# Seven products inside one of seven: a second level of the scheme for a12·b21, running sums kept in PSUM, and other steps for the scatters and gathers of the attention stage

## The chip, the cores and the metric

The kernel runs on one core of one Trainium2 chip, as a single program. The metric is the device time of one execution in microseconds (us). Three executions of the kernel before took 925.46, 924.17 and 926.12 us; the median is 925.46 us.

## The reference: what is computed

Two blocks follow each other, both in fp32. First, attention with a threshold, for 8 batches, 8 heads, 576 tokens and 64 features per head; second, a mixture of 8 experts in which a hash of the token's id picks the one expert that handles it.

```python
# attention: q, k, v are (8, 8, 576, 64), tau = 0.02
scores = scale * np.matmul(q, k.transpose(0, 1, 3, 2))
thresh = np.max(scores, axis=-1, keepdims=True) - tau
scores = np.where(scores >= thresh, scores, -1000000000.0)
scores = scores - np.max(scores, axis=-1, keepdims=True)
attn = np.exp(scores)
attn = attn / (np.sum(attn, axis=-1, keepdims=True) + 1e-09)
attn_out = np.matmul(attn, v)
# bridge: x is (4608, 512), a row for each token, the 8 heads side by side
x = attn_out.transpose(0, 2, 1, 3).reshape(B * S, H * D)
# experts: w1 is (8, 512, 1024), w2 is (8, 1024, 512)
expert_idx = token_ids * np.int64(2654435761) % np.int64(E)
for e in range(E):
    xe = x[expert_idx == e]
    out[expert_idx == e] = np.maximum(xe @ w1[e], 0.0) @ w2[e]
```

## The kernel before, in words

**Attention stage.** The work is cut into 32 pairs of heads (4 pairs of heads times 8 batches; index `p`), and each pair into five steps (`NS = 5`, index `s`, running number `n = 5p + s`). Step 0 handles the last 64 queries of both heads together, steps 1 to 4 handle 128 queries of both heads each. For each step TensorE computes scores into PSUM (`score`, L221 to L236), VectorE negates them into SBUF and keeps the row minimum (`negate`, L246), GpSimd adds the threshold to it (`thr`, L253), ScalarE takes the exponential (`expo`, L260), and one step later VectorE zeroes what is below the threshold and sums the rows (`mask`, L271). Two steps later TensorE turns the weights over (`turn_w`, L282), ScalarE copies them out of PSUM (`put_wT`, L298 and L303), and TensorE multiplies them with v (`av_part`, L313). At step 0 the result of the pair before last is turned back (`turn_o`), scaled by VectorE (`put_xm`, L352) and written by SyncE's (SP) queue into a DRAM tensor, `x_scratch` (L358 to L364). The order on every engine is the order of the code in the step loop (L710 to L805): nothing is reordered, so an instruction that waits holds all that is behind it on its engine.

**Routing beside it.** A generator `route` (L366) ranks the tokens in small pieces. When it is far enough (`placed`), `scatters` (L539) starts: 36 indirect DMAs that GpSimd issues, one whenever `next(scatter_pieces)` is called (L800 to L801), which is in steps 0, 2, 3 and 4. Loads of the sorted slots follow. At its end `routed` is set, and `fetch_early` (L677) may gather rows of `x_scratch` for expert 0: 15 indirect DMAs (5 tiles of tokens times the first 3 pairs of heads), one for each call. It is called at the start of step 0 (L713 to L714) and at the end of steps 3 and 4 (L802 to L803), once `n` is above `G0` = 130 (L671). Between the stages TensorE turns the gathered rows over (`early_xT`) and begins expert 0's first layer (`early_h`, `late_h`).

**Expert stage.** Each expert holds up to 600 tokens (544 for expert 0, 576 for experts 1 to 4, 600 for 5 to 7; their halves 272, 288 and 300 are the widths of the matmuls). Both layers are matrix products of 2 by 2 blocks, done with seven block products in place of eight (`seven`, L926): a11·b11, a12·b21, s2·t2, s3·t3, a22·t4, s1·t1 and s4·b22, where s1 to s4 and t1 to t4 are sums of blocks that VectorE makes beforehand (`left`, `right`, L863 to L872). A product is written into a PSUM tile of two banks. Four such tiles go round: two of the pool `ps_sc` and two of `ps_m`, taken in turn by `bank2` (L851). ScalarE copies p1 = a11·b11 to SBUF (L951); VectorE adds the other products to the running sums u2, u3, u4 in SBUF or to the outputs (L861). Layer 1 (L963) is done in two groups of 256 output features, so a12·b21 there is two products of eight matmul instructions each; layer 2 (L972) is one group, and a12·b21 is one product of sixteen instructions. (In the profile an fp32 matmul of the code is two MATMUL instructions, each with its weight load: L941 has four matmuls in a layer-1 product and eight records.) Layer 1 ends with a rectifier on ScalarE (L948).

**What runs beside the products.** `side1` and `side2` (L1093, L1107) hand out the other work after each product: the block sums of the next layer, the 32 by 32 transposes of gathered tokens (`turn_x`, L1060; VectorE then 16 DMAs on SP), the transposes of finished outputs (`put_squares`, L1029; VectorE, then up to ten indirect DMAs on GpSimd, each with a `pause` behind it, L1024: two copies of a small table, L1027, whose result is not read again), the gathers of the expert after next (`fetch`, L1051, with pauses too), and the loads of weights on SP. The weights of layer 2 are dealt (`dealt`, L877): the 128 columns of a weight load lie four elements apart, or two apart for the sums; expert 7's are not. After expert 7's layer 2 come the last 120 tokens (`last_tile`, L983), the last transposes and five indirect DMAs.

The functions that the diff touches and their callers:

## Time and profile before

| What | Value |
|---|---|
| median of three executions | 925.46 us (924.17 to 926.12) |
| the profiled execution, its own time | 926.27 us |
| its span | 924.6 us |
| attention, from the first negation to the end of pair 31's steps | about 7 to 462 us |
| expert 0's first layer, on TensorE | about 464 to 501.8 us |
| products of line L941 | 501.8 to 909.6 us |
| last tile and the last writes | 909.6 to 924.6 us |
| granted TensorE clock, mean | 0.999 |

Busy time is what an engine's instructions cover; the span is from the first instruction to the last. Times of rows in the timeline count from the start of the span. A releaser behind "<-" is what ended an engine's idle time as far as semaphores show it. Two executions of the kernel differ by about 0.1%, and the profiled one lies 0.8 us above the median.

### The profile page before, as it was taken

How to read it: one execution, taken by the hardware profiler on the slowest of the kernel's cores; microseconds unless marked ns; L12 is line 12 of the kernel's file. 1: busy time of each engine (PE TensorE's matmuls, PEld its weight loads, DVE VectorE, ACT ScalarE, POOL GpSimd, SP SyncE). 2: the span in 40 equal slices, each digit the busy share in tenths (PEclk: the TensorE clock that was granted, in tenths of full speed). 3: DMA queues.
4: the chain of work that ended last, by engine and by line, in shares of the span. 5: the costliest groups of instructions: out<-in, count | busy, mean ns of one | idle time of the engine just before them, and what ended most of it. 6: DMA issues, size and time to landing. Idle time of an engine off the chain costs nothing.

```text
span 924.6 us, 21039 instructions
## 1 busy us (share of the span) xinstructions
PE 906.9 (98%) x7495; PEld 661.6 (72%) x7495; DVE 759.9 (82%) x1654; ACT 457.3 (49%) x741; POOL 550.1 (59%) x842
## 2 busy tenths in 40 slices
PE   7999999999999999999999999999999999999997
PEld 4666666656666666565668879788887978879785
DVE  8999999999999999999945696867768685786741
ACT  6888888888888898788922020110202011020210
POOL 4233432456666623446414588787787877878773
PEclk9999999999999999999999999999999999999999
DMA  7454463554545668734011636445252543522001
GB/s 175 95 146 123 107 152 96 134 134 101 124 100 149 167 164 220 209 96 108 16 33 56 195 118 185 136 125 196 63 199 90 170 155 90 218 61 67 28 28 62
DMA packets 114777, 113.13 MB, mean 122 GB/s; under 512 B 32475, under 2 KB 89315, under 8 KB 114672
## 3 DMA queue, kind: packets, MB, share of 16 engines
q1 hardware_dynamic: 105168, 92.64, 37.0%
q0 software_dynamic: 9072, 18.91, 6.6%
q8 instruction: 61, 1.00, 0.4%
q14 instruction: 44, 0.36, 0.1%
q10 hardware_dynamic: 432, 0.21, 0.1%
HBM read 81.99 MB, written 21.44 MB: 112 GB/s over the span
## 4 chain that ended last, share of the span: by engine, by line
PE 83%; POOL 6%; issue 4%; DVE 3%; ACT 2%; DMA 1%; SPq 0%; POOLq 0%; DVEq 0%; ACTq 0%
PE bank L941 18%; PE av L313 18%; PE sc L941 18%; PE sc L235 14%; PE tr L282 11%; POOL out_dram L1042 4%; PE sc L640 3%; POOL stok_odd L1027 2%; PE av L282 1%; DVE ns L246 1%; DVE w L271 1%; ACT w L260 1%; DMA k_sb<-in_k_dram 1%; ACT wT_b L303 1%; PE bank L658 0%
## 5 line engine op out<-in xcount | busy, mean ns | idle before, releaser
L260 ACT ACTIVATE w<-ns,nmx 128x576 f32<-128x576 f32 x288 | 220.4, 776 | 28.6 <-DVE ns L246 27.9
L271 DVE SCALAR_TENSOR_TENSOR w<-ns,thr,w 128x576 f32<-128x576 f32 x288 | 225.7, 816 | 0.0
L253 POOL TENSOR_SCALAR thr<-nmx,drop 128x2 f32<-128x2 f32 (+1 forms) x160 | 104.4, 652 | 188.9 <-DVE ns L246 179.1
L246 DVE TENSOR_SCALAR_CACHE_REDUCE ns<-sc 128x576 f32<-128x576 f32 x288 | 205.7, 746 | 8.5 <-PE sc L235 7.7
L235 PE MATMUL sc<-k_sb,q 64*128 64x288 f32 (+1 forms) x1280 | 178.2, 422 | 1.1 <-DVE ns L246 0.6
L282 PEld LDWEIGHTS tr<-ident,w 64*128 64x128 f32 x2624 | 105.6, 138 | 96.9 <-ACT wT_b L303 35.3
L1042 POOL DMA_INDIRECT out_dram<-o_q,qidx x127 | 139.7, 1100 | 57.8 <-issue 49.2
L282 PE MATMUL tr<-ident,w 64*128 64x64 f32 x2624 | 139.2, 230 | 7.7 <-ACT wT_b L303 4.8
L1027 POOL COPY stok_odd<-stok 128x152 int32<-128x152 int32 x314 | 139.9, 445 | 10.0
L948 ACT ACTIVATE h<-h 128x576 f32<-128x576 f32 (+1 forms) x56 | 38.8, 693 | 142.8 <-DVE h L861 142.0
L235 PEld LDWEIGHTS sc<-k_sb,q 64*128 64x128 f32 (+1 forms) x1280 | 92.2, 177 | 23.5 <-DVE ns L246 9.8
L313 PE MATMUL av<-wT_a,v 128*64 128x320 f32 (+1 forms) x704 | 100.4, 418 | 0.2
L303 ACT COPY wT_a<-tr 128x512 f32<-128x512 f32 (+1 forms) x128 | 81.7, 638 | 20.6 <-PE tr L282 20.1
L303 ACT COPY wT_b<-tr 128x512 f32<-128x512 f32 (+1 forms) x128 | 81.3, 635 | 18.2 <-PE tr L282 10.2
L313 PE MATMUL av<-wT_b,v 128*64 128x256 f32 x640 | 83.2, 389 | 0.0
L313 PEld LDWEIGHTS av<-wT_a,v 128*64 128x64 f32 x704 | 43.7, 136 | 29.0 <-DVE xm L352 0.7
L951 ACT COPY p<-bank 128x576 f32<-128x576 f32 (+2 forms) x11 | 7.0, 634 | 107.5 <-PE bank L941 102.5
L313 PEld LDWEIGHTS av<-wT_b,v 128*64 128x64 f32 x640 | 40.2, 136 | 18.8 <-issue 0.7
L119 POOL DMA_INDIRECT xg<-x_scratch,gidx_x x35 | 41.8, 1193 | 19.2 <-issue 9.3
L542 POOL DMA_INDIRECT slot_scratch<-tok,slot_i x36 | 44.9, 1247 | 9.5 <-issue 7.6
L951 ACT COPY p<-sc 128x576 f32<-128x576 f32 (+2 forms) x11 | 7.0, 637 | 84.7 <-PE sc L941 79.8
L941 PE MATMUL bank<-h,w_sb 128*128 128x288 f32 (+3 forms) x192 | 48.1, 404 | 0.0
(198 smaller groups left out, 1402.4 us busy)
## 6 DMA issues: line engine op xcount, KB each, us to landing
w_sb<-in_moe_w_dram SPq DMA_DIRECT2D x16, 2048.0 KB
q<-in_q_dram SPq DMA_DIRECT2D x62, 288.0 KB
v<-in_v_dram SPq DMA_DIRECT2D x32, 256.0 KB
x_scratch<-xm SPq DMA_DIRECT2D x32, 256.0 KB
xT<-xq SPq DMA_DIRECT2D x84, 80.0 KB
k_sb<-in_k_dram SPq DMA_DIRECT2D x31, 144.0 KB
k_sb<-in_k_dram SPq DMA_DIRECT2D x32, 112.0 KB
x_scratch<-xg SPq DMA_DIRECT2D x9, 256.0 KB
```

Source lines behind the costliest of these rows:

```text
L235: nc.tensor.matmul(sc[out_rows, i, 0:S2], lhsT=q_sb[rows, h, q0:q1], rhs=k_sb[rows, h], start=True, stop=True)
L246: nc.vector.tensor_scalar(out=ns[:].rearrange("p (i s) -> p i s", i=2), in0=sc[:, :, 0:S2], scalar1=-1.0, scalar2=None, op0=ALU.mult, op1= ...
L253: nc.gpsimd.tensor_scalar(out=thr[:, 0:j + 1], in0=stats[n][0][:, 0:j + 1], scalar1=drop[:], scalar2=None, op0=ALU.add)
L260: nc.scalar.activation(w, nss[n, j][:], AF.Exp, bias=stats[n][0][:, j:j + 1], scale=-1.0)
L271: nc.vector.scalar_tensor_tensor(out=w, in0=nss.pop((n, j))[:], scalar=stats[n][1][:, j:j + 1], in1=w, op0=ALU.is_le, op1=ALU.mult, accum_ ...
L282: nc.tensor.transpose(dst[:, r, 64 * c:64 * c + 64], src[rows, c0:c0 + P], ident[rows, rows])
L303: nc.scalar.copy(dst, tr[:, :, 0:64 * n_c].rearrange("p r (c q) -> p r c q", c=n_c))
L313: nc.tensor.matmul(av[64 * j:64 * j + 64, g, c0:c1], lhsT=v_sb[:, c, 64 * j:64 * j + 64], rhs=wT[g][:, i, c0:c1], start=(c == 0), stop=stop)
L542: nc.gpsimd.indirect_dma_start(out=slot_dram[c % 2][:, :], out_offset=bass.IndirectOffsetOnAxis(ap=slot_i[:, c:c + 1], axis=0), in_=tok[:, ...
L941: nc.tensor.matmul(ps[:, i, 0:width], lhsT=lhsT, rhs=y[:, c], start=c == 0, stop=c == n_k - 1)
L1027: nc.gpsimd.tensor_copy(stok_odd[:], stok[:])
L1042: inst = nc.gpsimd.indirect_dma_start(out=rows[:, :], out_offset=bass.IndirectOffsetOnAxis(ap=idx, axis=0), in_=o_sb, in_offset=None, boun ...
```

## The change

Five things change together.

1. `Quarters`: the product a12·b21 of every layer of experts 1 to 7 is itself cut into 2 by 2 blocks and done by seven products of half the width (136 to 150 columns, 120 in expert 7's second layer). Its sums are made by VectorE in `inner_w` (in place and in `wi_s`) and `inner_b` (`bi_s`); for dealt weights ScalarE first copies a12 to a contiguous tile `w2_q` (`copy_quarters`). In layer 1 the two groups' products a12·b21 become one `Quarters` of 28 instructions; expert 0 keeps the plain product.
2. Sums in PSUM: in `Seven` and `Quarters`, u2 = p1 + s2·t2, u3 and c21 are added up by matmuls that go on writing into the tile that holds the earlier sum (`start=False`), after ScalarE or VectorE has copied the intermediate value out of it. c12 goes on in s1·t1's tile in the same way. The tile u4 goes away, and the four PSUM tiles get fixed roles (`banks`).
3. The step lists of `side1` and `side2` are new; `put_squares(e, 0)` moves from step 3 of layer 2 into the middle of its last product, and for expert 0 into expert 1's layer 1.
4. `pause` makes one copy, not two. Outputs of the last tiles use the gather tiles `xg_bufs`, not a pool of their own.
5. In the attention stage, the scatters are issued in steps 0 to 3 (before: 0, 2, 3, 4), and `fetch_early` is called at the end of steps 2 and 3, and of step 4 in pairs 25 and 26 alone. `G0` is 125, so the first gather is at n = 127 (before 133) and the fifteenth at n = 157, step 2 of pair 31 (before 155, step 0 of pair 31).

The core of the diff:

```diff
         LAST = NS * NP
-        G0 = NS * ((HP - 1) * B + 2)
+        G0 = NS * ((HP - 1) * B + 1)
         early = [(kt, hp) for kt in range(KT) for hp in range(HP - 1)]
...
-                if s == 0:
-                    fetch_early(n)
                 if s == 0 and p + 2 < NP:
...
-                if s != 1 and placed:
+                if s < NS - 1 and placed:
                     next(scatter_pieces, None)
-                if s > 2:
+                if s in (2, 3) or s == 4 and n < G0 + 2 * NS:
                     fetch_early(n)
...
-        w2_s = m_s.tile([P, 3, FH, D2], FP32, name="w2_s")
+        w2_s = m_s.tile([P, 2, FH, D2], FP32, name="w2_s")
+        w2_q = m_s.tile([P, 4, 2, P], FP32, name="w2_q")
...
+        banks, turn = [], [2]
...
+        def bank2():
+            turn[0] += 1
+            return banks[(turn[0] - 1) % 4]
...
-            t = triple(w2_s, 0, FH)
-            return t if e == E - 1 else [dealt(x, C2) for x in t]
+            t = [w2_s[:, i] for i in range(2)]
+            if e == E - 1:
+                return [*t, w_tiles["s4"]]
+            return [*(dealt(x, C2) for x in t), w2_blocks(e, w_tiles[e, 2])[1]]
...
-        def seven(a, a_s, b, b_s, m0, outs, relu, after):
...
+        def products(ps, x, y, start, mid=None):
+            for i, lhsTs in enumerate(x):
+                for c, lhsT in enumerate(lhsTs):
+                    nc.tensor.matmul(ps[:, i], lhsT=lhsT, rhs=y[:, c], start=start and c == 0,
+                                     stop=c == len(lhsTs) - 1, skip_group_check=not start)
+                if i == 0 and mid:
+                    mid()
...
+            def first(self):
+                products(self.x, self.a[0], self.b[0], True)
+            def keep_p1(self):
+                nc.scalar.copy(self.p1, self.x)
+            def second(self, y):
+                y = y[:, :, 0:self.x.shape[2]]
+                products(y, self.a[1], self.b[2], True)
+                self.out(self.outs[0], y, self.p1)
+            def u2_sum(self):
+                products(self.x, self.a[4], self.b[4], False)
+                nc.scalar.copy(self.u2, self.x)
+            def s1_t1(self, keep):
+                products(self.z, self.a[2], self.b[1], True)
+                if keep:
+                    nc.scalar.copy(self.mid, self.z)
+            def u3_sum(self, keep):
+                products(self.x, self.a[5], self.b[5], False)
+                if keep:
+                    nc.scalar.copy(self.mid, self.x)
+            def c21(self):
+                products(self.x, self.a[3], self.b[6], False)
+                if self.relu:
+                    nc.scalar.activation(self.outs[2], self.x, AF.Relu)
+                else:
+                    nc.scalar.copy(self.outs[2], self.x)
+            def c12(self, mid=None):
+                products(self.z, self.a[6], self.b[3], False, mid)
+                self.out(self.outs[1], self.z, self.u2)
+            def c22(self, ps):
+                self.out(self.outs[3], ps, self.mid)
+            def c11(self, p1):
+                self.out(self.outs[0], p1, self.outs[0])
...
+            def p1_p2(self):
+                products(self.x, self.a[0], self.b[0], True)
+                nc.scalar.copy(self.p1, self.x)
+                products(self.y, self.a[1], self.b[2], True)
+            def c11(self):
+                add(self.outs[0], self.y, self.p1)()
+            def p5_u2(self):
+                products(self.z, self.a[2], self.b[1], True)
+                nc.scalar.copy(self.p5, self.z)
+                products(self.x, self.a[4], self.b[4], False)
+                nc.scalar.copy(self.u2, self.x)
+            def c12_c22(self):
+                products(self.z, self.a[6], self.b[3], False)
+                add(self.outs[1], self.z, self.u2)()
+                products(self.x, self.a[5], self.b[5], False)
+                add(self.outs[3], self.x, self.p5)()
+            def c21(self):
+                products(self.x, self.a[3], self.b[6], False)
+                nc.scalar.copy(self.outs[2], self.x)
...
+        def copy_quarters(e):
+            w = w2_blocks(e, w_tiles[e, 2])[1]
+            nc.scalar.copy(w2_q[:].rearrange("p (i j) k m -> p i (j k) m", i=2),
+                           w.rearrange("p k m i -> p i k m"))
+        def w2_quarters(e):
+            if e == E - 1:
+                return w_quarters(w2_blocks(e, w_tiles[e, 2])[1])
+            return [w2_q[:, i] for i in range(4)]
...
+        def second_blocks(e, layer):
+            if layer == 1:
+                return w_quarters(w1_blocks(w_tiles[e, 1])[1]), x_blocks(e)[2]
+            return w2_quarters(e), h_blocks(0, FH, half2(e))[2]
+        def quarters_of(e, layer, x, y, z):
+            a_q, b = second_blocks(e, layer)
+            t = b.shape[2] // 2
+            if layer == 1:
+                outs = [h_0[:, 2 * i:2 * i + 2, t * k:t * k + t] for i in range(2) for k in range(2)]
+            else:
+                outs = [oT[:, i:i + 1, t * k:t * k + t] for i in range(2) for k in range(2)]
+            if (e, layer) == (E - 1, 2):
+                a_q[2] = w_tiles["s1_q"]
+            return Quarters(a_q, wi_sums(a_q[0]), b_quarters(b), bi_sums(b), outs,
+                            3 - layer, x, y, z)
...
+            q = quarters_of(e, 1, *banks[1:])
+            g0, g1 = group(0, banks[0], banks[2]), group(1, banks[1], banks[3])
+            w_tiles.pop((e, 1))
+            g0.first()
+            g0.keep_p1()
+            side(0)
+            q.p1_p2()
+            q.c11()
+            g0.u2_sum()
+            side(1)
+            q.p5_u2()
+            g0.s1_t1(True)
+            side(2)
+            q.c12_c22()
+            side(3)
+            g0.u3_sum(False)
+            q.c21()
+            g0.c22(g0.x)
+            side(4)
+            g0.c12()
+            g0.c11(g0.p1)
+            g1.first()
+            g0.relus()
+            side(5)
+            g1.c11(g1.x)
+            g1.relus()
+            g0.c21()
+            side(6)
+            g1.u2_sum()
+            side(7)
+            g1.s1_t1(True)
+            side(8)
+            g1.u3_sum(False)
+            side(9)
+            g1.c22(g1.x)
+            g1.c12()
+            g1.relus()
+            side(10)
+            g1.c21()
...
+            o = Seven(a, w2_sums(e), h_blocks(0, FH, half), triple(h_s, 0, FH, half), 0, outs,
+                      False, *((banks[0], banks[1]) if e else (banks[3], banks[2])))
+            o.first()
+            o.keep_p1()
+            if e == 0:
+                o.second(banks[0])
+                run(w2_first)
+                side(0)
+                o.u2_sum()
+                side(1)
+                o.s1_t1(True)
+                side(2)
+                o.u3_sum(False)
+                o.c22(o.x)
+                side(3)
+                o.c12()
+                side(4)
+                o.c21()
+                return
+            q = quarters_of(e, 2, *(banks[i][:, 0:1] for i in (2, 3, 3)))
+            q.p1_p2()
+            q.c11()
+            run(inner_b(second_blocks(e, 2)[1]), 4)
+            o.u2_sum()
+            q.p5_u2()
+            side(0)
+            o.u3_sum(True)
+            side(1)
+            q.c12_c22()
+            o.s1_t1(False)
+            side(2)
+            q.c21()
+            o.c11(o.p1)
+            o.c22(o.z)
+            o.c21()
+            side(3)
+            o.c12(lambda: side(4))
...
         def pause():
-            for _ in range(2):
-                nc.gpsimd.tensor_copy(stok_odd[:], stok[:])
+            nc.gpsimd.tensor_copy(stok_odd[:], stok[:])
...
-            run(sums_w2(0), 4)
+            w2_first = sums_w2(0)
+            run(w2_first, 3)
...
+            late_h(late_tile)
+            for _ in range(2):
+                banks += [ps_sc.tile([P, 2, 512], FP32, name="sc"),
+                          ps_m.tile([P, 2, 512], FP32, name="bank2")]
...
+                    a, b = second_blocks(e, 2)
...
+                    w2_work += inner_w(a, None if more else w_tiles["s1_q"])
+                    def side1(step):
+                        if step == 0 and e == 1:
+                            put_squares(0, 0)
+                        if step == (0 if e > 1 else 4):
+                            put_squares(e - 1, 1)
+                        if step == 2 and more:
+                            copy_quarters(e)
+                        run(w2_work, ((0, 1, 2, 0, 3, 1, 1, 0, 0, 0, 0) if e > 1 else
+                                      (0, 1, 2, 0, 0, 0, 1, 0, 1, 1, 0))[step])
+                        run(h_work, 2 if step in (8, 9) else 0)
+                        run(turns, ((0, 0, 0, 0, 0, 0, 1, 2, 1, 1, 1) if e > 1 else
+                                    (0, 0, 0, 0, 0, 1, 1, 1, 1, 2, 0))[step])
                     layer1(e, side1)
                     run(sums_h(e, 2, FH), 4)
...
+                    x_work = [sums_w1(e + 1), sums_x(e + 1), inner_w(a), inner_b(b)]
+                    if e == 0:
+                        x_work[1:3] = x_work[2:0:-1]
+                    x_work = sum(x_work, [])
...
-                    else:
-                        run(x_work, 2)
+                    run(x_work, ((1, 2, 3, 10, 0) if e else (2, 2, 0, 4, 8))[step])
                     if step == 2 and e + 2 < E:
                         fetch(e + 2)
                     if step == 4 and e + 2 < E:
                         load_w1(e + 2)
-                    if more and step == 3:
+                    if more and e and step == 4:
                         put_squares(e, 0)
```

Of the parts that are cut: `columns` picks the 128-column weights of a product; `left` and `right` are unchanged; `w_quarters` and `b_quarters` cut a block in four. A layer-1 product of `Seven` is eight instructions, a layer-2 product sixteen, and every product of `Quarters` four.

## The prediction

> **What bounds the kernel now.** I read the page's busy shares first, then busy times by stretch, the chain of work that ended last in order of time, the groups by form, and the timeline of single pairs.
>
> ```profile
> PE 906.9 (98%) x7495; PEld 661.6 (72%) x7495; DVE 759.9 (82%) x1654; ACT 457.3 (49%) x741; POOL 550.1 (59%) x842
> ...
> PEclk9999999999999999999999999999999999999999
> ```
>
> TensorE (PE) covers the span at full clock. The stretches of one expert's two layers show no gap at all:
>
> ```profile
> 602.00:627.00 25.00, 25.00 (x104) 22.00 (x104) 16.24 (x22) 2.69 (x4) 20.21 (x32) 1.00 0.55 160
> 627.00:653.00 26.00, 26.00 (x109) 21.59 (x108) 21.62 (x25) 2.70 (x4) 19.08 (x29) 1.00 0.40 136
> ```
>
> The columns are PE, PEld, DVE, ACT, POOL: PE 100%, DVE 65 to 83%, ACT 10%. In the chain's order of time the products follow each other without a break:
>
> ```profile
> 609.27 3.88 PE sc L941 x16
> 613.15 3.88 PE bank L941 x16
> ...
> 636.43 1.94 PE bank L941 x8
> 638.37 1.94 PE sc L941 x8
> ```
>
> So here an instruction costs its pitch: 3.88/16 = 1.94/8 = 242.5 ns at width 288. The same chain gives 252.5 at 300 (2.02/8), 229.4 at 272 (3.67/16), and the starts of expert 7's layer 2 give 202.5 at 240. All are width/1.2 + 2.5 ns. What is taken from PE in this stage is won, if no wait takes its place.
>
> In the attention stage DVE and PE are both nearly full. A pair takes 13.89 us, from one pair's first L246 row to the next's, in pairs 23 to 26. Pairs 14 to 22, which have scatters, take 14.35 on average (14.19 to 14.65), and pairs 27 to 30, with gathers, 15.96, 14.26, 14.11 and 15.78. Pair 27 in the timeline:
>
> ```profile
> 386.77 1.35 POOL L119 DMA_INDIRECT xg<-x_scratch,gidx  x1 [0.17 <-issue]
> ...
> 388.43 1.02 POOL L119 DMA_INDIRECT xg<-x_scratch,gidx  x1 [0.30 <-issue]
> ...
> 389.49 0.81 POOL L253 TENSOR_SCALAR thr<-nmx,drop 128x1 f32<-128x1 f32 x1
> 389.89 0.58 ACT L303 COPY wT_b<-tr 128x512 f32<-128x512 f32 x1 [1.81 <-PE sc L235]
> ...
> 390.53 0.52 PE L282 MATMUL tr<-ident,w 64*128 64x64 f32 x10 [1.58 <-ACT wT_b L303]
> ...
> 393.81 0.76 DVE L246 TENSOR_SCALAR_CACHE_REDUCE ns<-sc 128x576 f32<-128x576 f32 x1 [1.30 <-PE sc L235]
> ```
>
> The gathers of steps 4 and 0 run back to back over the start of step 0. ACT's wait for a turn that PE finished about 388 ends only at 389.8, then PE is 1.58 us late and DVE 1.30. Pair 30 looks the same. With scatters, the growth sits in step 0 alone: 3.2 us between its negation and the next, against 2.89, and only after a scatter in step 4; scatters in steps 2 and 3 leave their steps at 2.16 and 2.42, as in pair 23.
>
> **What the Trainium skill says.** "TensorE: Matmul & The Clock Gate", LDWEIGHTS (loading the stationary operand): a load takes its 128 columns / 1.2, so 107 ns, whatever the rows, and it overlaps matmuls. The trace agrees: after a break two loads start 108 ns apart (906.23, 906.34), and the last tile's 128-wide matmuls with 120-column weights run at 109 ns. The page has no price for dealt weights; these rows have:
>
> ```profile
> L941 PEld LDWEIGHTS bank<-h,w_sb 128*128 128x128 f32 x192 | 46.7, 300 | 0.5
> ...
> L941 PEld LDWEIGHTS bank<-xT,w_sb 128*128 128x128 f32 x168 | 31.9, 190 | 9.5
> ```
>
> Four elements apart lengthen a load from 190 to about 308 ns, and expert 0's products with such weights have a pitch of 233.75 (3.74/16) where 229.4 is normal: 234 is the load's own pace. "PSUM — Partial Sum Buffer", The four PSUM rules: a synchronised read of a sum in the middle of its group is allowed. No run here shows it yet. "SBUF — State Buffer" has GpSimd and VectorE share a port; the trace can't split that from a wait.
>
> **The change, part by part.** The sum stands against the profiled execution, 926.27 us (span 924.6 plus 1.7 around it), 0.8 above the median.
>
> *Quarters.* Per layer, 16 wide instructions go and 28 narrow ones come. At width 144 I extrapolate 144/1.2 + 2.5 = 122.5 ns (bounds: 121 by proportion; 190, a load's whole record, if loads don't overlap; the 109 ns row excludes the latter). Experts 1 to 4: 16 x 242.5 - 28 x 122.5 = 3.88 - 3.43 = 0.45 us a layer, eight layers, 3.6. Width 150: 4.04 - 28 x 127.5 = 0.47, five layers, 2.35. Expert 7's second: 3.24 - 28 x 109 = 0.19. Sum **-6.1** (bounds -6.7 and -5.5).
>
> *Dealt weights after a narrow product.* In layer 2, s1·t1 and a22·t4 begin behind 122 ns matmuls with a 234 ns load: 2 x 0.11 x 6 experts = **+1.3** (0 to 1.5). The narrow products themselves use contiguous w2_q. That copy, 1024 elements, is about 1.1 us of ACT (row L303: 585 ns for 512, 692 for 640), which is idle there.
>
> *Sums in PSUM.* Now PE waits for a copy before it adds on. Layer 1: after p1, PE has 4 + 4 narrow instructions, 0.98 us. ACT starts 0.24 after PE's last (638.21 to 638.45), copies 0.63 (row p) and PE follows 0.05 later: 0.92. It fits by 0.06 us, but the next weight load can no longer be ahead, so up to 0.11 shows. Layer 2 has this twice (p1, and u2 under p5 and u2 of the quarters). Three places by seven experts by 0.06: **+1.2** (0 to 2.3). The other reads are DVE's. I laid out expert 2 by hand: products at the pitches above, DVE items at 0.75 (adds), 1.22 (w sums), 2.26 (put_squares) and 0.69 (turn_x), the new quarter sums at 0.3 to 0.45 in proportion. Latest are the reads before q.c21 (1.3 us in hand), g1.u2_sum (0.8) and g1.c21 (0.9). None stalls; expert 1, with both put_squares in its layer 1, is about 0.4 late once: **+0.4** (0 to 1.5). Behind such a wait stands all of PE. DVE's load hardly changes: seven adds a group become three, and 16 quarter sums come.
>
> *Start of expert 0's layer 2.* Its first product goes into banks[3], the tile of late_h's last output. DVE reads that at 501.83 for 0.72, while PE is free at 501.80: **+0.85** (0 to 1). The fourth w2 sum moves behind the second product, and no PE work waits for it before c12.
>
> *Pauses, o_sb tiles.* One 445 ns copy less per row: POOL's rows come every 1.6 us, not 2.1. POOL stands in the chain late (839 to 905), but the last output waits for ACT at 918.0, POOL having been free from 917.5: 0. The writes are denser; weights have one expert's time to land. put_squares(e, 0) moves past load_w1 and one product: 2.3 us of DVE ahead of c12's add, 10 indirect DMAs later on POOL, under the next layer's first product; without that cover 2 us each. Expert 0's two blocks go to steps 0 and 4 of expert 1's layer 1, behind which DVE's w2 sums wait; the 0.4 above holds them. turn_x's 16 DMAs leave SP about 23 us into layer 1, 0.6 each, and their first reader comes 15 us into layer 2: 0.
>
> *Expert stage: -6.1 + 1.3 + 1.2 + 0.4 + 0.85 = -2.4.*
>
> *Scatters to step 1.* 36 x 1.25 us of POOL stay. Step 4's growth, 0.33 to 0.46 in each of nine pairs, 4.1 in all, can go. Step 1 on POOL: rec 0.5, scale_k 0.75, thr 0.73, then the scatter, with thr of step 2 queued behind it and DVE's mask behind that, a step later; from pair 26's rows it ends (380.0) before that thr is ready (about 380.6). If it costs what step 4's did, nothing is won. I take **-2** (-4.1 to 0).
>
> *Gathers.* Those of step 0 and three of five in step 4 go to steps 2 and 3, where a DMA of POOL costs nothing in the rows. The excess of pairs 27 to 30 is 2.07 + 0.37 + 0.22 + 1.89 = 4.55; two gathers in step 4 stay (0.35 each); half a us for what is left: **-3.3** (-4.5 to 0). New is that a gather follows the x_scratch writes of step 0 by two steps, not three: in pair 30 SP issues them 4 us into the pair, the gather comes about 8.5 in. The fifteenth, in step 2 of pair 31 (about 455), is needed at 464.8.
>
> Total -2.4 - 2 - 3.3 = **-7.7**: 926.3 - 7.7 = 918.6 profiled, 917.8 as a median; I say **918**.
>
> **The rivals.**
> (A) The sum holds: 918, between 913.5 and 922.5. For it: PE's pitch law and the fitting ledger.
> (B) The attention stalls stay, because SP's loads at step 0, or POOL's work wherever it is put, cause them: 925.5 - 2.4 = 923. For it: the named releaser, PE, had long been done, so the cause isn't seen; pairs 29 and 31 have gathers in step 0 and lose almost nothing.
> (C) Slower: PE is tied to DVE in layer 1. Before, a product had three other tiles' time (over 5.8 us) before its tile was needed; now g1.u2_sum and g1.c21 have 0.8. If DVE's items run 10% longer beside POOL (x_s 0.92 against 0.76 at 629.4 is such a case), the list up to these reads, some 12 us, is 1.2 late: 0.4 at each, and as much at q.c21 and in layer 2, plus the three copies at 0.3: 2.5 us an expert, 17.5 in all, 925.5 - 7.7 + 17.5 = 935. It decides from 1.4 us an expert on (7.7 + 1.9 over seven).
> (D) No change: a gain and stalls of 0.8 to 1.3 us an expert cancel, 925.5.
>
> **How the numbers follow.** Chances: A 0.57, B 0.17, C 0.15, D 0.11. The bounds add up to -6.7 to +0.8 in the expert stage and -8.6 to 0 in attention; all of them at their best would be 910, which I don't expect at once. A, B and half of D fill 912.5 to 925.5, with about 0.8 of the chance; C and the rest are left out. A measurement tells 0.2%, 1.85 us, from no change. Faster by more: A, and B but for 0.03: 0.72. Within: D and that, less a little: 0.12. Slower: C and a little of D: 0.16.
>
> **What would show it.** Right: narrow instructions at 122 to 128 ns; PE without gaps over 0.15 us from 503 on; an expert's two layers (288 wide) in about 53.8 us, before 54.3; a gap of 0.8 at expert 0's first product; pairs 14 to 22 near 13.95, and 27 to 30 near 14. Wrong: PE waiting for DVE's h L861-type adds by over 1 us an expert, narrow instructions above 140 ns, or step 0 still at 3.2 us with scatters in step 1.

## The result, and the profile after

| | before | after |
|---|---|---|
| median, us | 925.06 (9 executions, 923.99 to 926.43) | 919.05 (9 executions, 917.92 to 922.48) |
| ratio, 95% interval | | 0.9945 (0.9931 to 0.9959) |
| profiled execution, us (span) | 926.27 (924.6) | 919.58 (918.0) |
| pairs 14 to 22, over nine times 13.89 | 4.12 | 1.51 |
| pairs 25 to 30, over six times 13.89 | 4.56 | 4.12 |
| from pair 31's start to the end ("the last stage" below) | 477.35 | 473.37 |

The forecast was 918.0, so the total is hit within 1.1 us, and in part by luck: its two halves aren't. The expert stage was to give 2.4 us and gave about 4.0; attention was to give 5.3, and in the profiled executions pair 31 starts 2.7 us earlier (444.6 against 447.3; the pairs of the table won 3.0). The two misses, 1.6 and 2.6 us, have opposite signs. The page of the kernel after, busy times and clock, and the group of the pause (at the right: busy us and mean ns):

```profile
PE 902.9 (98%) x7663; PEld 669.3 (73%) x7663; DVE 758.8 (83%) x1720; ACT 514.0 (56%) x848; POOL 489.8 (53%) x685
...
PEclk9999999999999999999999999999999999999999
...
L1232 POOL COPY stok_odd<-stok 128x152 int32<-128x152 int32 x157 | 71.3, 454 | 0.6
```

PE has 168 instructions more and 4.0 us less to do; ACT has 56.7 us more, most of it copies out of PSUM; POOL lost half its pauses. Busy times by stretch over two experts' 54 us each (columns PE, PEld, DVE, ACT, POOL):

```profile
604.00:658.00 54.00, 54.00 (x251) 47.29 (x250) 40.97 (x59) 15.40 (x26) 37.04 (x45) 1.00 0.45 143
658.00:712.00 54.00, 54.00 (x251) 47.29 (x250) 40.78 (x59) 15.42 (x27) 40.15 (x49) 1.00 0.47 147
```

PE is still without a gap, DVE at 76%, where the kernel before had 74% in the first of these stretches (39.91 us). Layer 2 of expert 2 in the timeline, PE alone (start, duration, instructions):

```profile
609.28 0.65 PE L937 MATMUL sc<-h,w_q 128*128 128x144 f32 x4
609.77 0.65 PE L937 MATMUL bank<-h,w_q 128*128 128x144 f32 x4
610.26 4.07 PE L937 MATMUL sc<-h_s,w_s 128*128 128x288 f32 x16
614.17 0.66 PE L937 MATMUL bank<-h,w_q 128*128 128x144 f32 x4
614.66 0.65 PE L937 MATMUL sc<-bi_s,wi_s 128*128 128x144 f32 x4
615.15 4.12 PE L937 MATMUL sc<-h_s,w_s 128*128 128x288 f32 x16
619.11 0.65 PE L937 MATMUL bank<-h,wi_s 128*128 128x144 f32 x4
619.60 0.65 PE L937 MATMUL sc<-bi_s,wi_s 128*128 128x144 f32 x4
620.09 4.15 PE L937 MATMUL bank<-h,w_sb 128*128 128x288 f32 x16
624.07 0.66 PE L937 MATMUL sc<-bi_s,w_q 128*128 128x144 f32 x4
624.57 4.15 PE L937 MATMUL sc<-h_s,w_sb 128*128 128x288 f32 x16
628.55 0.65 PE L937 MATMUL bank<-h,w_sb 128*128 128x288 f32 x2
```

Read the starts: durations overlap. Four narrow instructions take 0.49 us (609.28 to 609.77), 122.5 ns each. The wide products with dealt `w_sb` behind narrow ones take 3.98 (620.09 to 624.07, 624.57 to 628.55), where 16 x 242.5 ns is 3.88. The two running sums take 3.91 and 3.96.

In attention, the waits of the kernel after in pairs 25 to 27 (us in total, times, longest) show what wasn't there before:

```profile
POOL xg L119 <- DVE ns L246: 15.0, 5, 5.5
...
DVE w L271 <- POOL thr L253: 4.0, 3, 1.8
```

DVE waits for a threshold that POOL computes, and POOL waits up to 5.5 us with a gather. POOL's timeline in pair 25 (which begins at 357.2):

```profile
363.83 0.73 POOL L253 TENSOR_SCALAR thr<-nmx,drop 128x2 f32<-128x2 f32 x1 [1.43 <-DVE ns L246]
369.37 1.13 POOL L119 DMA_INDIRECT xg<-x_scratch,gidx  x1 [4.81 <-DVE ns L246]
370.55 0.31 POOL L253 TENSOR_SCALAR thr<-nmx,drop 128x2 f32<-128x2 f32 x1
371.02 1.65 POOL L119 DMA_INDIRECT xg<-x_scratch,gidx  x1 [0.17 <-issue]
```

The gather of step 2 stands at POOL's head from 364.6 to 369.4, with the threshold of step 3 queued behind it. The releaser named (DVE) had long been done, so another wait was meant. A gather reads `x_scratch` and so waits for the pair's writes to it. SP issued those at 362.0 and they landed about 368.4; SP's own waits from 350 to 403 us say why they were late:

```profile
SPq L358 <- DMA xg<-x_scratch,gidx: 7.8, 2, 4.0
SPq L212 <- DMA w_sb<-in_moe_w_dram: 5.2, 2, 3.1
```

The second row is a load of `v` that, as the profile has it, waits in SP for the weights' DMA, and the writes stand behind it; the first is the writes themselves waiting for the gathers of the pair before, so late gathers in one pair also delay the next pair's writes. The 2 MB load of weights was issued at 352.8, ahead of all of them. From here my theory: these loads cost the gathers their gain. Rivals: two steps are too few for the writes whatever else is in the queue; or the gathers' own work on POOL is the cost.

### The profile page after: what moved, and what is told of

Same layout as the page of the kernel before. It is cut to its first block, busy times and chain, and to the rows that moved or that the text cites. A ratio compares the mean times of both kernels' runs of the same rounds, so it can differ in the third digit from the quotient of the medians.

```text
span 918.0 us, 21463 instructions
## 1 busy us (share of the span) xinstructions
PE 902.9 (98%) x7663; PEld 669.3 (73%) x7663; DVE 758.8 (83%) x1720; ACT 514.0 (56%) x848; POOL 489.8 (53%) x685
## 4 chain that ended last, share of the span: by engine, by line
PE 49%; POOL 27%; issue 15%; DVE 3%; ACT 2%; SPq 1%; DMA 1%; POOLq 1%; DVEq 0%; ACTq 0%
PE av L313 18%; POOL out_dram L1247 16%; PE sc L235 15%; PE tr L282 11%; POOL stok_odd L1232 8%; POOL xg L119 3%; PE sc L640 3%; PE av L282 1%; SPq L1277 1%; ACT w L260 1%; DMA k_sb<-in_k_dram 1%; DVE ns L246 1%; ACT wT_a L303 1%; DVE w L271 1%; POOLq L1247 0%
## 5 line engine op out<-in xcount | busy, mean ns | idle before, releaser
L1247 POOL DMA_INDIRECT out_dram<-o_q,qidx x127 | 147.2, 1159 | 114.4 <-DVE o_q L1238 81.2
L253 POOL TENSOR_SCALAR thr<-nmx,drop 128x2 f32<-128x2 f32 (+1 forms) x160 | 100.2, 626 | 173.9 <-DVE ns L246 162.4
L1232 POOL COPY stok_odd<-stok 128x152 int32<-128x152 int32 x157 | 71.3, 454 | 0.6
L937 PE MATMUL bank<-h,w_sb 128*128 128x288 f32 (+4 forms) x248 | 62.0, 402 | 0.0
L937 PEld LDWEIGHTS bank<-h,w_sb 128*128 128x128 f32 x248 | 58.7, 290 | 0.5
L937 PE MATMUL sc<-h_s,w_s 128*128 128x288 f32 (+2 forms) x224 | 56.6, 406 | 0.0
L961 ACT ACTIVATE h<-h 128x576 f32<-128x576 f32 (+1 forms) x42 | 29.0, 692 | 41.4 <-DVE h L864 36.3
```

The costliest lines, as they stand in the source:

```text
L253: nc.gpsimd.tensor_scalar(out=thr[:, 0:j + 1], in0=stats[n][0][:, 0:j + 1], scalar1=drop[:], scalar2=None, op0=ALU.add)
L937: nc.tensor.matmul(ps[:, i], lhsT=lhsT, rhs=y[:, c], start=start and c == 0, stop=c == len(lhsTs) - 1, skip_group_check=not start)
L1232: nc.gpsimd.tensor_copy(stok_odd[:], stok[:])
L1247: inst = nc.gpsimd.indirect_dma_start(out=rows[:, :], out_offset=bass.IndirectOffsetOnAxis(ap=idx, axis=0), in_=o_sb, in_offset=None, boun ...
```

## The experiments

They ran on three chips, called A, B and C. "Last stage" is from pair 31's start to the end in the profiled execution; it is free of the attention stage. "14-22" and "25-30" are these pairs' time above 13.89 us each, in the same execution. The executions of the section before are called those of the first chip.

| run | chip | median us | ratio to before, same chip (95%) | 14-22 | 25-30 | last stage |
|---|---|---|---|---|---|---|
| before | B | 925.59 | | 3.11 | 4.46 | 477.5 |
| after | B | 918.20 | 0.9914 (0.9894 to 0.9934) | 2.21 | 4.05 | 473.8 |
| after, old scatter steps | B | 920.74 | 0.9941 (0.9923 to 0.9959) | 3.60 | 3.83 | 473.3 |
| after, old gather steps | B | 918.53 | 0.9921 (0.9903 to 0.9938) | 1.22 | 4.19 | 473.6 |
| before | A | 918.21 | | | | |
| after, all old steps | A | 914.54 | 0.9959 (0.9945 to 0.9973) | -0.01 | 0.30 | 473.6 |
| before, new steps only | A | 920.90 | 1.0026 (1.0015 to 1.0037) | -0.01 | 2.18 | 477.6 |
| after, early weights | A | 913.71 | 0.9952 (0.9939 to 0.9966) | 0.00 | 0.16 | 473.3 |
| after, eight products | A | 925.27 | 1.0074 (1.0060 to 1.0088) | -0.01 | 3.16 | 480.0 |
| before | C | 918.14 | | | | |
| after, early weights | C | 913.96 | 0.9956 (0.9942 to 0.9969) | 0.01 | 0.15 | 473.7 |
| after, delay before c11 | C | 935.20 | 1.0189 (1.0174 to 1.0205) | -0.01 | 1.58 | 492.9 |
| after, delay behind c11 | C | 926.58 | 1.0105 (1.0081 to 1.0129) | 0.01 | 0.60 | 484.0 |
| after, two pauses | C | 929.41 | 1.0109 (1.0085 to 1.0132) | 0.01 | 3.75 | 489.2 |

**All steps old, and the steps alone (chip A).**

```diff
-        G0 = NS * ((HP - 1) * B + 1)
+        G0 = NS * ((HP - 1) * B + 2)
...
+                if s == 0:
+                    fetch_early(n)
...
-                if s < NS - 1 and placed:
+                if s != 1 and placed:
...
-                if s in (2, 3) or s == 4 and n < G0 + 2 * NS:
+                if s > 2:
```

> The kernel after with the scatters and gathers put back to their old steps. If the attention stage gave what its pairs show (pairs 14 to 22 won 2.6 us, pairs 25 to 30 won 0.4), this loses 3.0 us: about 922. If the attention stage gave what I had forecast (5.3), 924.3; if the whole gain is the expert stage's, 919. Pairs 25 and 26 should be back at 13.9 us, pair 27 at about 16.

The second kernel is the one before with the same lines the other way round.

> The kernel before with only the new steps of scatters and gathers. Theory (the two stages add up): 925.1 - 3.0 = 922. Rival (the moved transfers help only because expert 0's work then starts in another place, or hurt the expert stage): 925 or 919. Pairs 25 to 27 should show the new stalls in step 4 here too (about 1.3, 0.9 and 1.9 us), since the weights' loads are the same.

Both went against every number that I had given: on this chip the kernel before takes 918.2, the old steps are the faster ones (914.5), and the new steps alone make the kernel before 2.7 us slower. What holds is the sum of parts. The last stage is 473.6 with the new expert stage and 477.6 with the old, as in the first traces (473.4, 477.35), so the expert stage gives 4.0 us on either chip. The new steps' stalls come with the new steps: pair 27 takes 16.05 us in the second kernel, pairs 25 and 26 13.9. The old steps' stalls are missing here: pairs 14 to 22 take 13.89 each, pair 27 takes 14.04 and pair 30 13.89.

What differs can be seen in one place. ACT and POOL near 202.5 us, kernel before, first chip:

```profile
202.44 0.78 ACT L260 ACTIVATE w<-ns,nmx 128x576 f32<-128x576 f32 x1
203.74 0.58 ACT L303 COPY wT_b<-tr 128x512 f32<-128x512 f32 x1 [0.53 <-PE sc L235]
```

```profile
202.14 1.30 POOL L542 DMA_INDIRECT slot_scratch<-tok,slot_i  x1 [0.17 <-issue]
```

The same two engines with all old steps on chip A:

```profile
202.34 0.78 ACT L260 ACTIVATE w<-ns,nmx 128x576 f32<-128x576 f32 x1
203.11 0.59 ACT L303 COPY wT_b<-tr 128x512 f32<-128x512 f32 x1
```

```profile
202.03 1.30 POOL L542 DMA_INDIRECT slot_scratch<-tok,slot_i  x1 [0.17 <-issue]
```

POOL issues the same scatter at the same time, and PE's turn begins its last instruction at 202.88 in the first and 202.79 in the second. ACT's copy of it begins 0.86 us after that in the first and 0.32 in the second. Over pairs 14 to 22, ACT, when it has waited, begins such a copy 0.32 us after the turn's last instruction begins wherever POOL issues no indirect DMA at that moment; where it issues one, the median is 0.65 (at most 1.19) in the kernel before on the first chip, 0.62 on chip B, and 0.32 (at most 0.32) with the same steps on chip A. In the kernel after on the first chip, which still loses 1.5 us in pairs 16 to 21, it is 0.53.

The trace also records when PE's semaphore, its signal to the others, was raised. In the first execution the signals of three PE instructions that ended at 202.86, 203.11 and 203.65 came almost together, at 203.57, 203.66 and 203.72, just after POOL's DMA had ended at 203.44. On chip A they came at 202.78, 203.03 and 203.58, each within 0.03 us of its instruction's end, while POOL's DMA ran until 203.34. So ACT isn't slow: PE's signal itself is late while POOL issues an indirect DMA, on the first chip and on B, and on A and C it isn't. Why is open. Each of A, B and C was used in one set of runs only, so the chip can't be told from anything else that differed between the sets.

**Weights early (chips A and C).**

```diff
-                if s == 2 and p in (20, 24):
-                    load_w1(p // 4 - 5)
-                if s == 2 and p in (22, 26):
-                    load_w2((p - 22) // 4)
+                if s == 2 and p in (16, 20):
+                    load_w1(p // 4 - 4)
+                if s == 2 and p in (18, 22):
+                    load_w2((p - 18) // 4)
```

> The kernel after with the four 2 MB weight loads of experts 0 and 1 four pairs earlier (pairs 16, 18, 20, 22 for 20, 22, 24, 26), so that none shares the DMA queue with gathers. Theory (the x_scratch writes that the gathers of pairs 25 to 27 wait for stand behind a 2 MB load in the queue): writes land within about 5 us of the pair's start, pairs 25 to 27 go back to 13.9 us, 4.1 us are won, 915. Rival 1 (a gather two steps after the writes is too early whatever the queue carries, since SP issues the writes behind the pair's own loads): unchanged, 919. Rival 2 (the loads only move their stalls to the pairs with scatters): pairs 16 to 22 lose what pairs 25 to 27 win, 918 to 919.

Pairs 25 to 27 took 13.89, 13.89 and 14.05 us, pairs 16 to 22 stayed at 13.89: 913.71, and the five executions lie between 913.61 and 914.25. POOL in pair 25 of this kernel:

```profile
361.88 0.73 POOL L253 TENSOR_SCALAR thr<-nmx,drop 128x2 f32<-128x2 f32 x1 [1.43 <-DVE ns L246]
363.97 1.13 POOL L119 DMA_INDIRECT xg<-x_scratch,gidx  x1 [1.36 <-issue]
365.15 0.94 POOL L253 TENSOR_SCALAR thr<-nmx,drop 128x2 f32<-128x2 f32 x1
366.25 1.09 POOL L119 DMA_INDIRECT xg<-x_scratch,gidx  x1 [0.16 <-issue]
367.83 0.71 POOL L253 TENSOR_SCALAR thr<-nmx,drop 128x2 f32<-128x2 f32 x1 [0.50 <-DVE ns L246]
```

The same gather in the same step now begins 2.1 us after the threshold's start, not 5.5, and in SP's own waits the row `SPq L212 <- DMA w_sb` is gone. SP issues pair 25's writes 2.9 us into the pair, not 4.9, and they have landed 7.7 us into it, not 11.2. The theory's 915 had assumed a chip where after takes 919; what shows it right is pairs 25 to 30, with 0.16 us of stalls against 2.18 and 3.16 in the two runs on this chip that have the new gather steps and late weights. Both rivals fall: two steps are enough when the queue is free, and pairs 16 to 22 lose nothing. POOL's own work for the gathers costs at most 0.16 us here; where PE's signals are late this wasn't tried. Over all runs with new gather steps and late weights the stalls range from 0.60 to 4.12 us, presumably with when the 2 MB land against a pair; that would fit the spread of after, 917.92 to 922.48.

> The kernel after with the four early weight loads four pairs earlier, once more, for the chip of this call. Where before takes 918: 913.7, as measured. Where before takes 925: pairs 25 to 27 lose their stalls (4 us in after), the scatters' rest in pairs 16 to 21 stays (1.5 to 2 us): about 914.5 to 915, a ratio to before of 0.989.

The repeat came to chip C, where before takes 918.14: 913.96. On a chip where before takes 925 this version wasn't tried. The gain over all old steps is small where the signals are in time: 913.71 against 914.54 on chip A.

**Eight products in the quarters' block (chip A).** The edit, for layer 1 and layer 2 alike; `inner_w` and `inner_b` write their sums to tiles that nothing reads, ACT's copies of intermediate values go, and DVE copies results where it added (not shown):

```diff
-                products(self.x, self.a[0], self.b[0], True)
-                nc.scalar.copy(self.p1, self.x)
-                products(self.y, self.a[1], self.b[2], True)
+                products(self.y, self.a[0], self.b[0], True)
+                products(self.y, self.a[1], self.b[2], False)
...
+                products(self.z, self.a[0], self.b[1], True)
+                products(self.z, self.a[1], self.b[3], False)
...
+                products(self.x, self.a[2], self.b[1], True)
+                products(self.x, self.a[3], self.b[3], False)
...
+                products(self.x, self.a[2], self.b[0], True)
+                products(self.x, self.a[3], self.b[2], False)
```

> The kernel after with the quarters' block made of eight narrow products, two added up in each PSUM tile, in place of seven with inner sums; DVE's inner sums stay as work whose results nothing uses. PE gets 4 more instructions in each of 13 layers: 8 x 4 x 122.5 + 4 x 4 x 127.5 + 109 x 4 and so on, about 6.4 us, less 0.5 for the copies that nothing waits for now. Theory (expert stage bound by PE's pitch): 919.05 + 5.9 = 925. Rival (DVE bounds the layer since the change): 919 to 921.

The last stage went from 473.4 to 480.0, +6.6. I had counted 13 layers, there are 14: 56 narrow instructions more, eight layers at 122.5 ns, five at 127.5 and one at 109, are 6.9 us, from which go the waits that the copies may have caused. So in this stage added PE instructions cost nearly all of their time, and the rival, DVE, doesn't set the pace. The total, 925.27, looks like the forecast, but by chance: it assumed 919 for after, which on this chip would be about 917 (an estimate, see below).

**After, before, and one half of the steps each (chip B).**

> The kernel after, unchanged, next to the kernel before on the chip of this call. In the last call the kernel before took 918.2, not 925.1, and its old steps stalled nowhere (pairs 14 to 22 at 13.89, pair 27 at 14.04, pair 30 at 13.89), while the new steps kept their stalls in pairs 25 to 27. Theory 1 (the old steps' stalls belong to the chip, the new steps' to the kernel): where before takes about 918, after takes 918.2 - 3.7 (the expert stage) + 2.7 (new stalls) = 917.2, a ratio of 0.999; where before takes 925, 919. Theory 2 (after gains 0.55% wherever it runs): 913 where before takes 918.

> The kernel before, unchanged, for its profile on the chip of this call. If it takes about 918, Theory 1 expects pairs 14 to 22 at 13.89 us and pairs 27 to 30 near 13.9, and ACT's copy of a turned w beginning 0.1 to 0.2 us after PE's turn; if it takes 925, the stalls shown before (14.35 on average, 15.96 and 15.78) and that copy beginning only when PE's four score products have ended.

Chip B is of the kind where before takes 925, so theory 1's 919 applies: 918.20, a ratio of 0.9914. The six executions lie between 915.74 and 920.80, and theory 2's 0.55% would give 920.5 here, so this run doesn't decide between the two; chip A's runs speak for theory 1. The trace of before has the old stalls again (pair 27 15.97 us, pair 30 15.71).

```diff
-                if s < NS - 1 and placed:
+                if s != 1 and placed:
```

> The kernel after with the scatters alone back in their old steps (0, 2, 3, 4). On a chip where before takes 925: 2.6 us slower than after, in pairs 14 to 22. Where it takes 918: no difference from after (below 0.3 us), since the old steps stalled nothing there.

920.74 against 918.20: 2.5 us slower, near the 2.6 expected. But the executions overlap (919.43 to 922.14 against 915.74 to 920.80), so the size is uncertain. In pairs 14 to 22 the profiled executions with old scatter steps lose 3.11 and 3.60 us, those with new ones 2.21 and 1.22: the new steps win something there, 0.9 to 2.4 us.

```diff
-        G0 = NS * ((HP - 1) * B + 1)
+        G0 = NS * ((HP - 1) * B + 2)
...
+                if s == 0:
+                    fetch_early(n)
...
-                if s in (2, 3) or s == 4 and n < G0 + 2 * NS:
+                if s > 2:
```

> The kernel after with the gathers alone back in their old steps (3, 4 and 0, from one pair later on). Where before takes 918: 2.7 to 3.5 us faster than after, pairs 25 to 27 at 13.9 to 14.05, about 914.5. Where it takes 925: 0.4 us slower than after, the stalls in pairs 25 to 27 gone and those in 27 and 30 back.

918.53 against 918.20: no difference that these executions can show (expected 0.4). Pairs 25 and 26 are back at 13.89, pairs 28 and 30 at 15.41 and 15.78 (expected 27 and 30). On such a chip the gathers' new steps exchange one stall for another.

**How much PE has in hand at a DVE result (chip C).**

```diff
+            def extra():
+                w = min(half2(e - 1), half2(e))
+                for _ in range(2):
+                    add(h_s[:, 2, :, 0:w], h_s[:, 0, :, 0:w], h_s[:, 1, :, 0:w])()
...
+            extra()
             g1.c11(g1.x)
```

> The kernel after with two more DVE additions (0.75 us each, from parts of h_s into another part of it that nothing reads before it is written again) in each expert's layer 1, right before g1.c11, the addition that PE's g1.u2_sum waits for. In the trace of after DVE ends g1.c11 0.75 us before PE begins that product (expert 3: 648.71 and 649.46). Theory (in layer 1 PE has that much in hand at this read and no more): 1.5 - 0.75 = 0.75 us an expert, seven experts, +5.3 us in the stage from pair 31 to the end (473.4 in after), about 478.7. Rival (DVE's spare time, over 15% of the stage, takes it up as it did with the old order): 473.4.

935.20, far over the forecast. DVE and PE at that place:

```profile
649.98 2.85 DVE L864 TENSOR_TENSOR h_s<-h_s 128x1152 f32<-128x1152 f32 x2
652.75 0.75 DVE L864 TENSOR_TENSOR h<-bank,h 128x576 f32<-128x576 f32 x1
```

```profile
649.57 2.10 PE L937 MATMUL sc<-x_s,w_sb 128*128 128x288 f32 x8
653.56 0.76 PE L937 MATMUL bank<-x_s,w_s 128*128 128x288 f32 x2 [1.89 <-DVE h L864]
```

My edit was twice as large as I wrote: each addition had 1152 elements and 1.4 us, 2.85 together. Less the 0.75 in hand that is 2.1, and PE's eight instructions, due to last 1.94 us, are followed after 3.99: 2.05 late. The seven experts give 1.99, 2.06, 2.05, 2.09, 1.77, 1.88 and 1.38. The theory holds, at the right size. The stage lost more than these 13.2 us, 19.5, and most of the rest goes to the clock. Busy times by stretch around the stalls of experts 1, 2 and 6 (columns as above, PE's first; the third number from the end is the granted clock):

```profile
538.11:541.53 3.42, 1.91 (x8) 1.54 (x9) 3.42 (x5) 1.23 (x2) 3.25 (x3) 1.00 0.06 19
592.73:596.14 3.41, 1.52 (x7) 0.90 (x6) 3.38 (x4) 0.21 (x2) 3.17 (x3) 1.00 0.12 38
596.14:599.55 3.41, 3.41 (x8) 2.42 (x9) 3.31 (x7) 1.02 (x2) 3.07 (x5) 0.50 0.12 38
599.55:602.97 3.42, 3.42 (x15) 2.68 (x15) 2.63 (x4) 1.28 (x2) 3.13 (x4) 1.00 0.06 19
824.84:828.25 3.41, 1.70 (x8) 0.97 (x7) 3.38 (x6) 1.19 (x2) 3.07 (x4) 1.00 0.06 19
828.25:831.66 3.41, 3.41 (x15) 2.60 (x14) 3.31 (x6) 0.97 (x3) 3.07 (x5) 1.00 0.12 38
```

In the second row PE idles 1.89 us (0.16 less than it is late, since records of neighbouring instructions overlap by that). For the next 3.41 us it runs at half its pace, some 480 ns an instruction, which costs another 1.7 to 1.9 us. The same follows the stalls of experts 3 and 4. In expert 6 PE idles 1.71 us, and the clock stays. Expert 1's stall is longer, 1.83 us of idle, but it falls on two such stretches, 1.51 in the one shown, and the clock stays too; the last section has more on this.

> The same two additions one place later, right behind g1.c11. The next DVE result that PE waits for is c22's addition, read before g1.c21: DVE is busy from 648.97 to 655.10 without a pause, idles 0.45, and ends that addition 0.91 us before PE needs it. Theory: 1.5 - 0.45 - 0.91 = 0.14 us an expert at most, with the signal's time 0.2, so 1.0 to 1.4 us in all, stage 474.4 to 474.8. If the place doesn't matter, the same as the run before (478.7); if neither has a cost, 473.4.

The same call one line later cost 10.6 us in the last stage, against 19.5; the 474.8 at most that I expected is far off, again since the edit was twice as large. With the true 2.85 the expectation is 2.85 - 0.45 - 0.91 = 1.5 us an expert; PE was 1.2 late in experts 2 to 4, 0.95 and 1.2 in two later ones, 2.4 in expert 1 (where the clock halved once more), none in expert 7. So the place decides, and what counts is the distance to the next DVE result that PE waits for.

**Two pauses (chip C).**

```diff
-            nc.gpsimd.tensor_copy(stok_odd[:], stok[:])
+            for _ in range(2):
+                nc.gpsimd.tensor_copy(stok_odd[:], stok[:])
```

> The kernel after with the second copy back in each pause between two rows that POOL puts out. Theory (POOL's rows end early enough): the stage stays at 473.4 us, no difference from after. Rival (POOL, which stands in the chain that ended last of after from 839 us on, sets the end): 32 rows of the last expert by 0.45 us at the worst, up to +14; at least +2.

The stage went to 489.2, +15.8, but not at the end, where the rival had put it. DVE and POOL between experts 3 and 4:

```profile
685.56 0.74 DVE L864 TENSOR_TENSOR oT<-bank,u 128x576 f32<-128x576 f32 x1
693.40 2.21 DVE L1239 STREAM_TRANSPOSE o_q<-oT 128x1152 f32<-128x1152 f32 x1 [7.10 <-DMA out_dram<-o_q,qidx]
```

```profile
685.63 0.98 POOL L1248 DMA_INDIRECT out_dram<-o_q,qidx  x1 [0.43 <-issue]
687.73 0.98 POOL L1248 DMA_INDIRECT out_dram<-o_q,qidx  x1 [0.43 <-issue]
```

The second `put_squares` of an expert writes `o_q` again, and waits for the rows of the expert before that POOL is still putting out until 688.7, and for their landing. DVE is held 7.1 us, and with it PE: it is 5.6 us late at 695.95 and 5.1 at 813.6, with 5.1 and 3.4 us at half clock behind, which makes about 15 of the 15.8. This execution was the slowest of four (925.65 to 933.10). With one pause, in the kernel after, POOL is through well before. Its waits between 640 and 700 us:

```profile
POOL out_dram L1247 <- DVE o_q L1238: 9.9, 1, 9.9
```

It idles 9.9 us until DVE has the next expert's first block ready. The second copy, 0.45 us in each of some 20 pauses an expert, takes 9 of that.

## Why the total was right and its halves wrong

- **Quarters, -6.1: right.** 122.5 ns at width 144, as extrapolated, and eight products in place of the seven cost 6.6 us more.
- **Dealt weights behind a narrow product, +1.3: right.** About 0.105 us twice in each of six experts, 1.3.
- **Sums in PSUM, +1.2: two thirds as large at most.** In layer 1 nothing shows. In layer 2 the running sums take 0.03 and 0.08 longer than their pitch. Over all products PE is some 2.1 us further behind the law (width/1.2 + 2.5) than before; less the 1.3 that is 0.8 with everything else in it. Whether those 0.11 are the copy or the load of `w_s`, two elements apart, isn't told apart.
- **DVE's reads, +0.4: 0.1.** Expert 1 shows 0.07 and 0.05. The ledger by hand was good: 1.3, 0.8 and 0.9 us in hand before q.c21, g1.u2_sum and g1.c21 are 1.28, 0.75 and 0.91 in the trace.
- **Start of expert 0's layer 2, +0.85: wrong, nothing.** The product begins at 498.79, 0.23 after late_h's last matmul and before DVE has begun to read that output (498.99), so it writes another tile. I had taken the order in which tiles are reused from the code, without a row that shows it.
- **Pauses, 0: right for the change, for a wrong reason.** I had looked at the last output alone. The cover that mattered is `o_q`'s next use, and with two pauses it costs 15.8 us under the new order, in the slowest execution.
- **Other moves, 0: right.** `put_squares(e, 0)` and `turn_x` leave no gap in PE.
- **Expert stage, -2.4: it was -4.0**; the terms above, -6.1 + 1.3 + 0.8, make it.
- **Scatters, -2: -2.6** in the first two profiled executions, 0.9 to 2.4 on chip B. The range of the forecast holds; the cause, late signals, wasn't in it. On A the old steps cost nothing, so there is nothing to win.
- **Gathers, -3.3: wrong, -0.4.** The step that failed is "in pair 30 SP issues them 4 us into the pair, the gather comes about 8.5 in". Pair 30 was the wrong pair to read it from: pairs 25 and 27 (the first gathers now come one pair and one step earlier) have a 2 MB load ahead of the writes in SP's queue, and in pair 25 the writes landed 11.2 us into the pair. I had the queue's order for the loads of a pair and left out the load of the weights. Where the signals are in time the new gather steps don't win at all: the kernel before gets 2.7 us slower by the new steps (chip A).

Rival B had a part of the truth: the stalls' cause wasn't seen. There are two, late signals under POOL's DMAs for the old steps and the weights' loads for the new ones. That the forecast gain came so close is luck on two counts: the misses of the two halves have opposite signs, and the chip was one with late signals. Rival C, PE tied to DVE, was possible, as the delays show, and wasn't met: 0.75 us was enough. On chips A and C the kernel after itself wasn't run. The new steps on the old expert stage (920.9) less the expert stage's 4.0 give an estimate of 916.9 there, a gain of 1.3 us and a ratio of 0.9986, where the chips with late signals give 0.9945 and 0.9914. The fastest version of those run there is after with early weights, 0.9952 and 0.9956 of before.

## What to carry to other kernels

When a DMA that waits for a write is moved closer to it, find what is in the write's queue in exactly the steps to which it goes, the large loads that come seldom included: one 2 MB load ate what the move had won. A stage bound by one engine is priced by that engine's pitch, but each read by another engine has its own time in hand; list these, since the same 2.85 us of work an expert cost 19.5 or 10.6 us in all, depending on a line. And work that only fills time on an idle engine may still be what a later buffer waits for.

## What the runs showed of the hardware

- While POOL issued an indirect DMA, PE's signal to ACT came 0.3 us later in the median, and in the pairs with gathers up to 1.9 us later, in the first traces and on chip B. With the same steps on chip A it didn't, nor on C with the new ones. The kernel before takes 925 where it is late and 918 where it isn't.
- In the expert stage the granted clock went to half for 3.41 us or twice that, and within a run always on one beat: with the delay before c11 such stretches begin at 596.14, 654.17 and 712.20, each 17 times 3.413 us apart, with two pauses at 694.26 and 813.73, 35 times 3.413. In the three kernels of chip C that delay PE, the clock fell after each of the six beats at full clock in which PE idled 1.88 us or more, and after none with 1.71 or less. So a stall of 2 us costs nearly 4 if it falls within one beat. Idle time alone isn't the whole rule: in the run with old scatter steps the clock fell at 18.15 us after a beat with 1.38 us of idle, and at the end of the run with two pauses it stayed at full after one with 1.93. The Trainium skill, "TensorE: Matmul & The Clock Gate", section "The HAM clock gate", has the clock go down after at least one idle window of about 3.4 us; here windows idle for little more than half of that sufficed.
- Behind each other without a wait, and with contiguous weights, fp32 matmul instructions stood width/1.2 ns plus 2.5 apart, from 144 columns (122.5) to 300 (252.5).
